# Opening the z1 stage before the last row's norm is finished

## The chip, the cores and the metric

The kernel runs on one core of one Trainium2 chip. The metric is the time of one execution on the device in microseconds (us); lower is better. The engines are named as in the profile: PE (TensorE, matmuls), PEld (its weight loads), DVE (VectorE), ACT (ScalarE), POOL (GpSimd) and SP (SyncE, which here only issues DMAs). Each engine has its own list of instructions and works through it in order; an instruction waits until the semaphores it names say that its operands are there and its buffer is free.

## The reference, cut to what matters

One block of an FNet mixer followed by a gated MLP, for x of 2048 rows by 512 columns, in float32:

```python
mod = (silu(c) @ w_mod).reshape(c.shape[0], 6, 1, -1)          # sa, ca, ga, sb, cb, gb
h = layernorm(x) * (1 + ca) + sa
x = x + ga * Real(DFT_seq(DFT_hidden(h)))                      # Cr @ a - Ci @ b
h = layernorm(x) * (1 + cb) + sb
z = gelu(h @ w_in)                                             # 2048 x 1792
z1, z2 = z[..., :896], layernorm(z[..., 896:])
g = w_sp @ z2 + b_sp                                           # w_sp is 2048 x 2048
x = x + gb * ((z1 * g) @ w_out)
```

## The kernel before, in words

Every float32 matmul is made of three matmuls on rounded parts: high by high, low by high, high by low (`matmul3`, lines 95 to 97). A high part is an ACT copy (`ah`, line 249), a low part is a DVE subtraction (`al`, line 265), each of 128 by 512 elements.

The work is a row of numbered chunks. Chunks 0 to 127 (`N2` is 128) are the DFT along the sequence: four quarters `t` of 512 output rows, in PSUM tiles `gp`. As a quarter ends, `mm_y` makes the DFT along the hidden dimension, four row tiles `yp` of 128 rows. Each row tile goes through five steps: `post_y` (DVE scales and adds x, then takes mean and variance; POOL stores x and finishes the statistics), `norm_y` (ACT applies them), `post_h` (DVE multiplies by `mod4` and adds `mod3`), `turn_h` (DVE turns the tile into `hturn`, POOL stores it to `ht_d` in DRAM with four DMAs). Chunks 128 to 155 (from `N2` to `N3`) make z1 from `ht_d` and the left half of w_in: 7 products of the Strassen-Winograd kind with 4 chunks each, tiles `z1p`, and a leftover column block `f7p` of 128 columns. Chunks 156 to 183 (`N3` to `N4`) make z2 the same way (`z2p`). Chunks 184 to 295 (from `N4`) make w_sp times z2 (`gw`), and the output product `op` follows.

The order on every engine is written by hand. In each chunk `prep(n)` emits the high part of chunk n+3 and the low part of chunk n+2, then the matmuls are emitted, then `run(n)` emits whatever `at(n, ...)` has put on that chunk's list. `prep_hi` and `prep_lo` for chunks 128 to 131 read `xb0`, the turned rows of quarters 0 and 1 that already lie in SBUF; chunks 132 to 135 read `xb1`; quarters 2 and 3 come back from `ht_d` through `load_t` into the tiles `tt2` and `tt3` of the pool `slots`, which `change_s` opens where the DFT's pools have been closed.

The place the change is about is the passage from chunk 127 to 128. There, the lists at `N2 - 0.25` hold the five steps of the last quarter's four rows, one row after the other. The first z1 chunks follow at once: `mm_z1(128)` (product 1, left pair), `mm_z1(130)` (right pair), `mm_z1(132)` (product 2, which begins with two `f7p` groups on chunks 132 and 133), and then `mm_x(0)`, the `f7p2` matmuls on `xh` and `xl`, parts of `tt2`. `empty_z1` copies a finished `z1p` tile to SBUF with ACT. `mm_x(0)` writes the PSUM bank that `f7p0` filled, so it waits for the gelu that empties it (line 670), the first gelu of the program, ahead of which ACT loads its table.

Tiles that share a tag share a ring of buffers: `row` has 6 in the pool `rows` (x rows, h rows, and in the last quarter the odd turned rows), `hturn` has one.

## Time and profile before

| | |
|---|---|
| runs shown (3) | median 950.87 us, 949.32 to 951.08 |
| the profiled execution | 949.74 us |
| its span in the trace | 948.0 us |
| PE busy | 934.8 us (99% of the span) |
| DVE busy | 737.5 us (78%) |
| ACT busy | 413.5 us (44%) |
| POOL busy | 196.2 us (21%) |
| mean granted PE clock | 0.997 |

The 1.7 us between the profiled time and the span lie outside the program's instructions. In a timeline row the columns are: start in us from the start of the span, duration in us, engine, line, operation, written tile <- read tiles, shape, count, and in brackets how long the engine was idle before it and what ended that. Matmuls overlap: one of 512 columns is listed with 0.39 us, but in an unbroken row the next starts 0.227 us later (0.203 us for 448 columns). What a wait costs is therefore read from start to start, less that step. In a waits row stand who waited, for whom, the total in us, how often, and the longest.

### The profile page before, as it was taken

The page shows a single profiled execution, that of the slowest core. Times are in us where ns is not written, and L with a number is a line of the kernel's source. Part 1 is how long each engine was busy: PE and PEld are TensorE (multiplying, and loading weights), DVE is VectorE, ACT ScalarE, POOL GpSimd, SP SyncE. Part 2 cuts the span into 40 slices and gives each one's busy share as a digit, 9 for nine tenths or more (in the row PEclk, how much of TensorE's full clock was granted, in tenths as well). Part 3 has the DMA queues.
Part 4 walks back from the last instruction along what each step waited for, and adds up shares of the span by engine and source line. Part 5 has one row for each costly group of instructions (what it writes and reads, how often), then busy time and mean ns, then how long its engine had stood idle before and what let it go on. Part 6 is the DMA issues. An engine that isn't in the chain of part 4 may idle for free.

```text
span 948.0 us, 12382 instructions
## 1 busy us (share of the span) xinstructions
PE 934.8 (99%) x4114; PEld 773.2 (82%) x4114; DVE 737.5 (78%) x1201; ACT 413.5 (44%) x725; POOL 196.2 (21%) x372
## 2 busy tenths in 40 slices
PE   8999999999999999999899999999999999999998
PEld 5888888888887888888688898888888888888886
DVE  7799957777667677866787868999799889886662
ACT  4694424232132222322577778765545444331221
POOL 2330000114544165323414211332000000000000
PEclk9999999999999999999999999999999999999999
DMA  9995752657448977994767322544555465744441
GB/s 209 221 224 122 137 145 67 167 140 195 121 120 235 325 224 213 278 336 158 230 246 271 140 82 57 149 92 102 135 131 122 101 156 126 185 101 156 180 175 56
DMA packets 236592, 157.07 MB, mean 166 GB/s; under 512 B 131472, under 2 KB 203408, under 8 KB 236400
## 3 DMA queue, kind: packets, MB, share of 16 engines
q1 hardware_dynamic: 223008, 118.65, 50.0%
q0 software_dynamic: 12128, 37.11, 10.9%
q8 instruction: 32, 0.52, 0.2%
q10 hardware_dynamic: 1392, 0.52, 0.2%
q14 instruction: 32, 0.26, 0.1%
HBM read 119.54 MB, written 36.70 MB: 165 GB/s over the span
## 4 chain that ended last, share of the span: by engine, by line
PE 86%; issue 6%; POOL 3%; DVE 3%; ACT 1%; DMA 1%; SPq 0%; POOLq 0%; DVEq 0%
PE gp L96 12%; PE gp L95 12%; PE gp L97 12%; PE gw L97 10%; PE gw L96 10%; PE gw L95 10%; PE op L97 3%; PE op L96 3%; PE op L95 3%; PE yp L97 2%; PE yp L96 2%; PE yp L95 2%; PE z2p L97 2%; PE z2p L96 2%; PE z2p L95 2%
## 5 line engine op out<-in xcount | busy, mean ns | idle before, releaser
L249 ACT ACTIVATE ah<-t 128x512 fp32r<-128x512 f32 x248 | 156.4, 631 | 373.1 <-DVE t L186 267.5
L265 DVE TENSOR_TENSOR al<-t,ah 128x512 fp32r<-128x512 f32 x248 | 166.7, 673 | 59.2 <-PE gp L96 32.8
L96 PE MATMUL gp<-al,hh 128*128 128x512 f32 x496 | 193.1, 389 | 0.9 <-DVE al L265 0.9
L95 PE MATMUL gp<-ah,hh 128*128 128x512 f32 x496 | 193.0, 389 | 0.0
L97 PE MATMUL gp<-ah,hl 128*128 128x512 f32 x496 | 193.0, 389 | 0.0
L186 DVE STREAM_TRANSPOSE t<-stage 128x512 f32<-128x512 f32 x240 | 168.6, 702 | 7.4 <-DMA stage<-in_A_dft_seq_re_dram 3.3
L97 PE MATMUL gw<-ah,bl 128*128 128x512 f32 x400 | 155.9, 390 | 0.3 <-DVE bl L806 0.3
L95 PE MATMUL gw<-ah,bh 128*128 128x512 f32 x400 | 155.7, 389 | 0.0
L96 PE MATMUL gw<-al,bh 128*128 128x512 f32 x400 | 155.6, 389 | 0.0
L96 PEld LDWEIGHTS gp<-al,hh 128*128 128x128 f32 x496 | 93.1, 188 | 20.5 <-DVE al L265 1.3
L95 PEld LDWEIGHTS gp<-ah,hh 128*128 128x128 f32 x496 | 93.1, 188 | 19.5
L97 PEld LDWEIGHTS gp<-ah,hl 128*128 128x128 f32 x496 | 93.1, 188 | 19.3
L97 PEld LDWEIGHTS gw<-ah,bl 128*128 128x128 f32 x400 | 75.1, 188 | 16.6 <-DVE bl L806 1.0
L95 PEld LDWEIGHTS gw<-ah,bh 128*128 128x128 f32 x400 | 75.1, 188 | 15.6
L96 PEld LDWEIGHTS gw<-al,bh 128*128 128x128 f32 x400 | 75.1, 188 | 15.6
L778 POOL DMA_DIRECT2D s_d<-sj x64 | 35.1, 548 | 97.0 <-DVE sj L770 81.2
L95 PE MATMUL yp<-hth,gh 128*128 128x512 f32 x128 | 49.8, 389 | 0.0
L96 PE MATMUL yp<-htl,gh 128*128 128x512 f32 x128 | 49.8, 389 | 0.0
L97 PE MATMUL yp<-hth,gl 128*128 128x512 f32 x128 | 49.8, 389 | 0.0
L569 POOL DMA_DIRECT2D ht_d<-hturn x62 | 40.9, 665 | 30.4 <-DVE hturn L565 26.2
L95 PE MATMUL op<-woh,uh 128*128 128x512 f32 x112 | 43.6, 389 | 0.0
L96 PE MATMUL op<-wol,uh 128*128 128x512 f32 x112 | 43.6, 389 | 0.0
(200 smaller groups left out, 1445.4 us busy)
## 6 DMA issues: line engine op xcount, KB each, us to landing
stage<-in_A_dft_seq_im_dram SPq DMA_DIRECT2D x64, 256.0 KB, 5.3
sj<-in_B_w_sp_dram SPq DMA_DIRECT2D x32, 512.0 KB, 7.4
s_d<-sj POOLq DMA_DIRECT2D x64, 256.0 KB, 3.7
stage<-s_d SPq DMA_DIRECT2D x128, 128.0 KB, 2.8
stage<-in_A_dft_seq_re_dram SPq DMA_DIRECT2D x60, 256.0 KB, 5.4
stage<-in_B_w_sp_dram SPq DMA_DIRECT2D x96, 128.0 KB, 3.0
wm<-in_w_mod_dram SPq DMA_DIRECT2D x16, 256.0 KB, 5.8
xr<-in_A_x_dram POOLq DMA_DIRECT2D x16, 256.0 KB, 4.6
```

Source lines behind the costliest of these rows:

```text
L95: nc.tensor.matmul(acc, ah, bh, start=first, stop=False, skip_group_check=go_on)
L96: nc.tensor.matmul(acc, ah, bl, start=False, stop=False, skip_group_check=go_on)
L97: nc.tensor.matmul(acc, al, bh, start=False, stop=last, skip_group_check=go_on)
L186: nc.vector.transpose(dst.rearrange("p (b i) -> p b i", i=32), block[:, :, 32 * k:32 * k + 32])
L249: nc.scalar.activation(AH[n], T[n], AF.Copy)
L265: nc.vector.tensor_tensor(AL[n], t, AH[n].bitcast(F32), op=ALU.subtract)
L569: eng.dma_start(v[a, i], ht[32 * a:32 * a + 32].rearrange("c (b r) -> c b r", r=32))
L778: nc.gpsimd.dma_start(s_d[m, r, g][b * P:(b + 1) * P, :], a)
```

## The change

Five things are changed.

1. `turn_h` puts the turned tile of every odd row of quarters 1 to 3 into the `row` ring. Before, only the last quarter did so, and all rows of quarters 0 to 2 shared the one `hturn` buffer.
2. In `mm_z1` the copies of the three `z1p` tiles are emitted ahead of the leftover matmuls of product 1, not behind them.
3. In the passage, the low part of chunk 131 is emitted ahead of `post_y` of the last row; `norm_y`, `post_h` and `turn_h` of the last row move behind `mm_z1(128)`, with the high parts of chunks 132 and 133 and the low part of 132 emitted between them. `change_s`, and with it the pool for `tt2`, moves behind them, and `load_t(2)` from the list of chunk 128 to that of 129.
4. The sums on w_in's right half: `form_w(6)` moves from chunk `N3` to `N2 + 26`, which is `N3 - 2`; `form_w(5)` and `form_w(4)` one chunk earlier.
5. The first eight z norms (`norm_z` on DVE and POOL, `scale_z` on ACT) move two chunks later, and `hi_b` of the first w_sp product one chunk later.

```diff
     def prep_hi(n):
-        if n >= NE:
+        if n >= NE or n in highs:
             return
+        highs.add(n)
...
-        pl, tag, n = (rows, "row", 6) if t == NQ - 1 and i % 2 else (GP_[0], "hturn", 1)
+        pl, tag, n = (rows, "row", 6) if t and i % 2 else (GP_[0], "hturn", 1)
...
+        for f in range(3):
+            empty_z1(p, gg, f)
         if p == 1:
             for kk, t in enumerate(a):
                 mm_f7(gg, kk, *t)
-        for f in range(3):
-            empty_z1(p, gg, f)
...
-                at(N2 - 0.25, post_y, t, i)
                 if i == 3:
                     at(N2 - 0.25, prep_lo, N2 + 3)
-                at(N2 - 0.25, norm_y, t, i)
+                at(N2 - 0.25, post_y, t, i)
                 if i:
                     at(N2 - 0.25, turn_h, t, i - 1)
-                at(N2 - 0.25, post_h, t, i)
+                if i < 3:
+                    at(N2 - 0.25, norm_y, t, i)
+                    at(N2 - 0.25, post_h, t, i)
...
-    change_s()
-    zout.append(w0.enter_context(pool("zout")))
-    at(N2, load_t, 2)
+    at(N2 + 1, load_t, 2)
...
+    at(N2 + 26, form_w, 6)
...
             mm_z1(n)
+            if n == N2:
+                prep_hi(N2 + 4)
+                norm_y(NQ - 1, 3)
+                prep_hi(N2 + 5)
+                prep_lo(N2 + 4)
+                post_h(NQ - 1, 3)
+                turn_h(NQ - 1, 3)
+                change_s()
+                zout.append(w0.enter_context(pool("zout")))
...
-        if p == 6:
-            at(N3, form_w, 6)
...
-    at(N3 + 6, form_w, 5)
-    at(N3 + 7, form_w, 4)
+    at(N3 + 5, form_w, 5)
+    at(N3 + 6, form_w, 4)
...
-            at(n - 4, hi_b, p, k)
+            at(n - (3 if p == 1 else 4), hi_b, p, k)
...
-                at(n - 7, norm_z, k)
-                at(n - 6, scale_z, k)
+                at(n - 5, norm_z, k)
+                at(n - 4, scale_z, k)
```

Neither PE's nor POOL's nor SP's list of instructions changes its order; on DVE and ACT the same instructions stand in another order at a few places. Three of them are shown.

ACT in the passage, before: `h2_3_3` is the last row's norm, the DMA two of its four stores, `z1_1_0x` and `z1_1_1x` the copies of product 1's left and right tiles, `ah132` to `ah134` the high parts of those chunks.

```order
L119 ACTIVATE h2_3_3_4235<-xr3_3_4183,nmry_4231,rsy_4228 128x512
L569 DMA ht_d3_83<-hturn3_3_4245 32x16x32 x2
L708 ACTIVATE z1_1_00_4302<-z1p1_00_4274 128x4x4x32
L708 ACTIVATE z1_1_01_4304<-z1p1_01_4281 128x4x4x32
L708 ACTIVATE z1_1_02_4306<-z1p1_02_4288 128x4x4x32
L249 ACTIVATE ah132_4308<-xb1_3935 128x512
L249 ACTIVATE ah133_4313<-xb1_3935 128x512
L708 ACTIVATE z1_1_10_4350<-z1p1_10_4322 128x4x4x32
L708 ACTIVATE z1_1_11_4352<-z1p1_11_4329 128x4x4x32
L708 ACTIVATE z1_1_12_4354<-z1p1_12_4336 128x4x4x32
L249 ACTIVATE ah134_4356<-xb1_3935 128x512
```

The same stretch of ACT's list in the changed kernel:

```order
L710 ACTIVATE z1_1_00_4262<-z1p1_00_4241 128x4x4x32
L710 ACTIVATE z1_1_01_4264<-z1p1_01_4248 128x4x4x32
L710 ACTIVATE z1_1_02_4266<-z1p1_02_4255 128x4x4x32
L252 ACTIVATE ah132_4275<-xb1_3935 128x512
L119 ACTIVATE h2_3_3_4277<-xr3_3_4183,nmry_4233,rsy_4230 128x512
L252 ACTIVATE ah133_4279<-xb1_3935 128x512
L571 DMA ht_d3_83<-hturn3_3_4285 32x16x32 x2
L710 ACTIVATE z1_1_10_4343<-z1p1_10_4322 128x4x4x32
L710 ACTIVATE z1_1_11_4345<-z1p1_11_4329 128x4x4x32
L710 ACTIVATE z1_1_12_4347<-z1p1_12_4336 128x4x4x32
L252 ACTIVATE ah134_4356<-xb1_3935 128x512
```

The left tiles' copies and `ah132` now stand ahead of the last row's norm, and `ah133` ahead of the two stores; the right tiles' copies and `ah134` still stand behind the stores.

DVE in the passage, before: `y3_3`, `xr3_3`, `bsty` and `mvy` are `post_y` of the last row, `hturn3_2` and `hturn3_3` the turned third and fourth row.

```order
L546 TENSOR_TENSOR y3_3_4220<-yp3_3_0_4099,mod2_1784 128x512
L547 TENSOR_TENSOR xr3_3_4183<-y3_3_4220,xr3_3_4183 128x512
L103 BN_STATS bsty_4224<-xr3_3_4183 128x6
L105 BN_AGGR mvy_4226<-bsty_4224 128x2
L265 TENSOR_TENSOR al131_4233<-xb0_3845,ah131_4188 128x512
L565 STREAM_TRANSPOSE hturn3_2_4237<-h2_3_2_4205 128x512
L557 TENSOR_TENSOR h2_3_3_4235<-h2_3_3_4235,mod4_2060 128x512
L558 TENSOR_TENSOR h2_3_3_4235<-h2_3_3_4235,mod3_2222 128x512
L565 STREAM_TRANSPOSE hturn3_3_4245<-h2_3_3_4235 128x512
L265 TENSOR_TENSOR al132_4315<-xb1_3935,ah132_4308 128x512
L265 TENSOR_TENSOR al133_4317<-xb1_3935,ah133_4313 128x512
```

And in the changed kernel:

```order
L267 TENSOR_TENSOR al131_4220<-xb0_3845,ah131_4188 128x512
L548 TENSOR_TENSOR y3_3_4222<-yp3_3_0_4099,mod2_1784 128x512
L549 TENSOR_TENSOR xr3_3_4183<-y3_3_4222,xr3_3_4183 128x512
L103 BN_STATS bsty_4226<-xr3_3_4183 128x6
L105 BN_AGGR mvy_4228<-bsty_4226 128x2
L567 STREAM_TRANSPOSE hturn3_2_4235<-h2_3_2_4211 128x512
L267 TENSOR_TENSOR al132_4281<-xb1_3935,ah132_4275 128x512
L559 TENSOR_TENSOR h2_3_3_4277<-h2_3_3_4277,mod4_2060 128x512
L560 TENSOR_TENSOR h2_3_3_4277<-h2_3_3_4277,mod3_2222 128x512
L567 STREAM_TRANSPOSE hturn3_3_4285<-h2_3_3_4277 128x512
L267 TENSOR_TENSOR al133_4317<-xb1_3935,ah133_4279 128x512
```

`al131` moved ahead of the last row's four statistics instructions, `al132` ahead of its last three; `al133` kept its place behind the last turn.

DVE in the last z2 product, four chunks ahead of `N4`, before: `t180` and `t181` are sums for chunks 180 and 181, `bstz` and `mvz` the statistics of the first z norm (`norm_z`), `z2_12` the first of four sums of a finished PSUM tile.

```order
L232 TENSOR_TENSOR t180_5436<-xb1_3935,s2_00_4430 128x512
L644 TENSOR_TENSOR wj2_5398<-w2_4310,wj2_5398 128x2x448
L103 BN_STATS bstz_5441<-z2_0_5158 128x6 x2
L105 BN_AGGR mvz_5444<-bstz_5441 128x2
L232 TENSOR_TENSOR t181_5451<-xb1_3935,s2_01_4435 128x512
L265 TENSOR_TENSOR al180_5455<-t180_5436,ah180_5438 128x512
L265 TENSOR_TENSOR al181_5457<-t181_5451,ah181_5453 128x512
L746 TENSOR_TENSOR z2_12_5028<-z2p5_4_5354,z2_12_5028 128x448
```

And in the changed kernel:

```order
L232 TENSOR_TENSOR t180_5436<-xb1_3935,s2_00_4430 128x512
L646 TENSOR_TENSOR wj2_5398<-w2_4314,wj2_5398 128x2x448
L232 TENSOR_TENSOR t181_5441<-xb1_3935,s2_01_4435 128x512
L267 TENSOR_TENSOR al180_5445<-t180_5436,ah180_5438 128x512
L267 TENSOR_TENSOR al181_5447<-t181_5441,ah181_5443 128x512
L748 TENSOR_TENSOR z2_12_5028<-z2p5_4_5354,z2_12_5028 128x448
```

The first norm's statistics left this place; they stand one list further on, behind `t182`, and ACT's `scale_z(0)` moved with them, from behind `ah181` to behind `ah183`.

More of the change, by code (lines that the diff above doesn't have):

```diff
@@ L234, in form_t @@
         return {7: c, 4: d, 5: a, 3: b}[p]
+    highs, lows = set(), set()
     def prep_hi(n):
-        if n >= NE:
+        if n >= NE or n in highs:
             return
+        highs.add(n)
         if N2 <= n < N4:
@@ L252, in prep_hi @@
             load(b + 2)
-    lows = set()
     def prep_lo(n):
@@ L1041, in fnet_gmlp_kernel @@
                     at(N2 - 0.25, prep, N2)
-                at(N2 - 0.25, post_y, t, i)
                 if i == 3:
                     at(N2 - 0.25, prep_lo, N2 + 3)
-                at(N2 - 0.25, norm_y, t, i)
+                at(N2 - 0.25, post_y, t, i)
                 if i:
                     at(N2 - 0.25, turn_h, t, i - 1)
-                at(N2 - 0.25, post_h, t, i)
+                if i < 3:
+                    at(N2 - 0.25, norm_y, t, i)
+                    at(N2 - 0.25, post_h, t, i)
                 if i < 2:
                     at(N2 - 0.25, load_xr, t, i + 2)
-                for f, *a in (((hi_v, 1), (lo_v, 1)), ((make_w7, 0),), ((hi_v, 2), (lo_v, 2), (make_w7, 1)), ((turn_h, t, 3),))[i]:
+                for f, *a in (((hi_v, 1), (lo_v, 1)), ((make_w7, 0),), ((hi_v, 2), (lo_v, 2), (make_w7, 1)), ())[i]:
                     at(N2 - 0.25, f, *a)
```

## The prediction

> **What bounds the kernel now.** I read the page's busy times first, then the waits of PE, then PE's timeline around each wait, then the engines that end them.

> ```profile
> PE 934.8 (99%) x4114; PEld 773.2 (82%) x4114; DVE 737.5 (78%) x1201; ACT 413.5 (44%) x725; POOL 196.2 (21%) x372
> ```

> PE is busy for 99% of the span and the change leaves its instructions and their order alone. So time can only be won or lost where PE waits. Its waits are few; the largest behind the start (who, for whom, total us, times, longest):

> ```profile
> PE f7p L95 <- ACT ah L249: 2.3, 1, 2.3
> PE z2p L95 <- ACT ah L249: 1.7, 2, 1.4
> ...
> PE z1p L96 <- DVE al L265: 1.0, 1, 1.0
> ```

> These, and two smaller ones shown below, lie at places that the change touches: `gp` in quarter 2, `z1p` and `f7p` in the passage, `z2p` at both ends of that stage, `gw` at its start. I cost them in order of time. Times below are those of the trace before; what earlier terms move is added at the end only.

> **Turned rows in the ring.** PE and DVE in quarter 2:

> ```profile
> 293.45 0.39 PE L95 MATMUL gp<-ah,hh 128*128 128x512 f32 x1
> 294.75 0.50 PE L96 MATMUL gp<-al,hh 128*128 128x512 f32 x1 [0.91 <-DVE al L265]
> ```

> ```profile
> 292.82 0.71 DVE L565 STREAM_TRANSPOSE hturn<-h 128x512 f32<-128x512 f32 x1 [3.92 <-DMA ht_d<-hturn]
> ```

> DVE stands for 3.92 us until the one buffer's stores have landed, and behind it stands the low part that PE lacks. PE loses 294.75 - 293.45 - 0.23 = 1.07 us. With odd rows in the ring the fourth turn needs no landing of the third, and 3.92 us of wait ahead of a loss of 1.07 leave a wide margin. The ring's other users, x rows loaded through POOL, have had this pattern in the last quarter already. Term: -1.07.

> **The passage.** PE there:

> ```profile
> 455.86 0.39 PE L95 MATMUL z1p<-ah,vj 128*128 128x512 f32 x1
> 457.21 0.50 PE L96 MATMUL z1p<-al,vj 128*128 128x512 f32 x1 [0.96 <-DVE al L265]
> 457.55 0.40 PE L97 MATMUL z1p<-ah,vj 128*128 128x512 f32 x1
> ...
> 461.69 0.39 PE L97 MATMUL f7p<-ah,w 128*128 128x512 f32 x1
> 464.39 0.49 PE L95 MATMUL f7p<-ah,w 128*128 128x512 f32 x1 [2.31 <-ACT ah L249]
> ...
> 468.58 0.40 PE L95 MATMUL z1p<-ah,vj 128*128 128x512 f32 x1
> ...
> 472.02 0.39 PE L95 MATMUL f7p<-xh,w 128*128 128x512 f32 x1
> ```

> From 455.86 to 457.55 two steps take 1.69, a loss of 1.24. From 461.69 to 468.58 ten steps of 0.227 take 6.89, a loss of 4.62. Together 5.86. The second loss is not the wait alone: the granted clock fell.

> ```profile
> 461.59:465.00 3.41, 0.98 (x4) 0.25 (x2) 0.63 (x2) 2.75 (x6) 1.29 (x2) 1.00 0.51 96
> 465.00:468.41 3.41, 3.30 (x8) 2.62 (x9) 3.38 (x6) 3.41 (x8) 0.00 (x0) 0.50 0.39 132
> 587.88:591.29 3.41, 1.92 (x9) 1.32 (x9) 2.41 (x5) 3.41 (x7) 1.33 (x3) 1.00 0.49 110
> ```

> (Columns: stretch, length, busy us and count of PE, PEld, DVE, ACT, POOL, granted clock, DMA share, GB/s.) Half clock ran from 465.00 to 468.41, after a stretch of 3.41 us in which PE was busy for 0.98 (29%). A stretch of the same length with 1.92 (56%) was not followed by it. Half clock cost 3.41 / 2 = 1.7 of the 5.86.

> What ends the two waits is ACT and DVE working for the last row first:

> ```profile
> 458.25 0.81 ACT L119 ACTIVATE h<-xr,nmry,rsy 128x512 f32<-128x512 f32 x1 [5.56 <-POOL nmry L115]
> 461.30 0.91 ACTq L569 DMA_DIRECT2D ht_d<-hturn  x2
> 462.25 1.57 ACT L708 ACTIVATE z<-z1p 128x512 f32<-128x512 f32 x3 [3.18 <-PE f7p L97]
> 464.73 1.58 ACT L708 ACTIVATE z<-z1p 128x512 f32<-128x512 f32 x3
> 470.43 0.60 ACT L670 ACTIVATE z1o<-f7p 128x512 f32<-128x512 f32 x1
> ```

> ```profile
> 446.56 0.69 DVE L265 TENSOR_TENSOR al<-xb,ah 128x512 fp32r<-128x512 f32 x1
> ...
> 459.10 0.69 DVE L557 TENSOR_TENSOR h<-h,mod 128x512 f32<-128x512 f32 x1 [1.32 <-ACT h L119]
> ...
> 460.55 0.71 DVE L565 STREAM_TRANSPOSE hturn<-h 128x512 f32<-128x512 f32 x1
> ```

> `al131` now stands four DVE instructions earlier and is done some 2 us before PE asks: the 1.24 go. `ah132` runs in the 5.56 us for which ACT waits at 458.25, and `al132` fills DVE's 1.32 at 459.10, since one low part is 0.69 long and lets the next start after 0.60 (two in a row take 1.29, below). Both cost nothing there. But `al131` pushes the last row's chain back by 0.60: turn at 461.15, stores at 461.90.

> What is late next, then. First `al133`, behind that turn: it starts some 0.6 later, at 461.8, and is done at 462.5. PE, without the 1.24, asks for it at 461.69 - 1.24 + 5 x 0.227 = 461.59: a new wait of 0.90. Then the `f7p2` matmuls, which stood at 472.02 and need the bank that the first gelu frees. From the second trio of copies (464.73) to that gelu's end (471.03) ACT works without a hole, 6.30 us: copies, two high parts, two `xh`, weights, table load, gelu. In the new order the right tiles' copies follow the stores directly, at 461.90 + 0.95 = 462.85, so the bank is free at 469.15 and PE goes on at 469.20. PE itself is there at 472.02 - 5.86 + 0.90 = 467.06, and waits about 2.1. So the passage is 472.02 - 469.20 = 2.8 shorter, less 0.1 for the slower first matmul behind a wait (457.21 to 457.55 is 0.34, not 0.23): -2.7. Two waits become two others, and the copies' place ahead of the leftover matmuls buys nothing, because the right ones wait for the stores. A sum that took the removed waits alone would give 5.9.

> That holds at full clock. The new wait leaves PE idle for about 2.0 us, so the fullest stretch of 3.41 around it has PE busy for 41%, between the 29% and the 56% above, and it lies wholly in one stretch in (3.41 - 2.0) / 3.41 = 41% of phases. I give half clock about 2 in 10, at a price of 1.7. [...]

> **w_in's sums.** At the start of z2:

> ```profile
> 530.57 0.95 ACT L640 ACTIVATE wj<-w 128x896 fp32r<-128x896 f32 x1 [3.09 <-DVE w L629]
> ```

> ```profile
> 533.23 0.36 PE L97 MATMUL z2p<-wj,al 128*128 128x448 f32 x1
> ...
> 534.86 0.36 PE L95 MATMUL z2p<-wj,ah 128*128 128x448 f32 x1
> ```

> ```profile
> 526.91 1.29 DVE L265 TENSOR_TENSOR al<-t,ah 128x512 fp32r<-128x512 f32 x2 [0.18 <-ACT ah L249]
> ...
> 529.45 1.08 DVE L629 TENSOR_TENSOR w<-w 128x896 f32<-128x896 f32 x1
> ```

> PE loses 534.86 - 533.23 - 4 x 0.203 = 0.82 behind ACT's 3.09 us wait for `form_w(6)`. Two chunks earlier the sum is ready and that wait is gone. On DVE its 1.08 now stand ahead of the low parts of chunks 158 and 159. Those ended at 527.6 and 528.2; PE began on that half 24 matmuls of 0.203 before 533.43, at 528.6, and read them from 529.0 and 529.6: 1.4 to spare, 0.3 left. Term: -0.8; if the cover were gone, up to 0.8 of it would come back.

> **z's norms.** The end of z2:

> ```profile
> 587.59 0.36 PE L97 MATMUL z2p<-wj,al 128*128 128x448 f32 x1
> ...
> 590.62 0.37 PE L96 MATMUL z2p<-wj,ah 128*128 128x448 f32 x1
> ...
> 595.64 0.50 PE L97 MATMUL gw<-ah,bl 128*128 128x512 f32 x1 [0.33 <-DVE bl L806]
> ```

> ```profile
> 583.95 1.14 ACT L119 ACTIVATE z<-z,nmrz,rsz 128x896 f32<-128x896 f32 x1 [0.89 <-POOL nmrz L115]
> ...
> 588.73 1.14 ACT L249 ACTIVATE ah<-t 128x512 fp32r<-128x512 f32 x2
> ...
> 590.29 1.12 ACT L119 ACTIVATE z<-z,nmrz,rsz 128x896 f32<-128x896 f32 x1
> ```

> ```profile
> 580.37 1.15 DVE L103 BATCH_NORM_STATS2 bstz<-z 128x6 f32<-128x448 f32 x2
> ```

> Loss: 590.62 - 587.59 - 5 x 0.203 = 2.0, and at 595.64 the 0.33 shown and 0.16 of overlap, 0.5, with 0.1 behind it: 2.6. Ahead of `ah182`, at 588.73, the change takes away a wait of 0.89 and a scale of 1.14 on ACT, and 1.15 of statistics on DVE ahead of that; `ah182` comes 1.2 to 1.9 earlier, at 586.8 to 587.5, done half of 1.14 later, by 588.1 at the latest, against PE's 587.79. The 2.0 shrink to 0.3. But the norm now stands between `ah183` and the first `bh`: its scale, then the copies and high parts that were there before, and `bl` comes behind them. Before, the scale began 583.95 - 580.37 = 3.6 behind the start of its statistics. Now these stand behind four sums of 0.55 and `t182` (0.6). The sums move with the pairs, and start at 582.5 to 583.1; so the scale starts at 588.9 to 589.5, where the second norm's stood at 590.29, with the same copies and high parts behind it and one `bh` of 0.5 more ahead of the last `al`. `bl` comes 0.3 to 0.9 earlier, up to 1.5 if POOL's part of the 3.6 is shorter here. PE asks 1.7 earlier, so its wait grows from 0.5 to between 0.7 and 1.9, and `bl` sets the term: between -0.3 and -1.5; I take -0.7, inside the nearer span. The other seven norms are still scaled four chunks ahead of their use, 48 matmuls of 0.227 or 10.9 us.

> **The sum.** -1.07 - 2.7 - 0.8 - 0.7 = -5.3. The profiled execution took 949.74 (span 948.0 and 1.7 around it), 1.1 under the median shown: 944.4 for it, 945.6 against the median of 950.87. POOL and SP keep their order, so no transfer is issued behind another that it stood ahead of.

> **Rivals.**
> - The new wait cools the clock: +1.7, 947.3. For it the 29% stretch, against it the 56% one. Still faster.
> - The passage is not shortened, because `tt2` comes late. SP's loads wait for buffers:

> ```profile
> SPq L205 <- PE yp L97: 17.4, 1, 17.4
> SPq L205 <- DMA ht_d<-hturn: 16.3, 1, 16.3
> ```

> The first is `load_t(2)`, which waits for `yp` matmuls, the second `load_t(3)`, issued at 465.9 when the last turned row has landed. The pool for both is now opened behind that row's turn. If the first load must wait like the second, `tt2` lands some 3.5 us later, at 469.4; 3.8 of ACT's 6.30 follow, and PE goes on at 473.3, 1.3 later than before instead of 2.8 earlier. Sum: 1.07 + 0.8 + 0.7 - 1.3 = 1.3 gained, 949.6: within 0.2%, which is 1.9 us and about what a measurement of this kernel can tell from no change. Against it: what it waited for in the end was PE, which the matmuls' operands under those buffers explain, and these stay where they were.
> - Slower, by DVE in the first w_sp product, where the norms now fall two chunks later and run into the second eight:

> ```profile
> 597.00:610.78 13.78, 13.78 (x63) 11.38 (x62) 13.18 (x25) 9.38 (x14) 4.75 (x9) 1.00 0.48 109
> ```

> DVE is busy for 13.18 of 13.78. That leaves 0.24 in each pair of chunks (24 matmuls of 0.227, 5.4 us). One more norm's statistics in each of the 8 pairs, 1.15, would put 0.9 a pair on PE, 7.3 in all: 945.6 + 7.3 = 952.9. It decides once more than 5.3 of it reach PE. Against it: of the first eight norms three instead of four now stand ahead of that product, so one is added, not eight, and PE waits nowhere in that stretch.

> **How the numbers follow.** Forecast 0.65; clock 0.19; late `tt2` 0.09; DVE 0.07. Faster by over 0.2%: 0.84; within: 0.09; slower: 0.07. The forecast's own bounds are the norm term (0.4 up, 0.8 down) and the runs' spread (949.32 to 951.08). The range takes the clock rival in with the norm term at its worst end, 945.6 + 1.7 + 0.4 and 0.9 of spread, 948.6; below, the norm term at its best and the profiled execution for the base, 943.6, with 0.4 for new waits taken too long: 943.2.

> **What would show it.** Right: no PE wait in quarter 2; PE's first z1 wait on `al133`, about 0.9; a wait of about 2 on the gelu ahead of `f7p2`, with full clock behind it; none at `form_w(6)`; a wait on `bl` of about 1.3 at the first `gw`. Wrong: half clock after the passage, SP's first `L205` waiting on `hturn`, or PE waiting for `al` in the first w_sp product.

## The result and the profile after

The changed kernel takes 945.69 us (median of 4 runs, 944.42 to 946.25), the kernel before, in the same comparison, 950.8 (4 runs, 949.32 to 951.08): a ratio of 0.9948, 95% interval 0.993 to 0.9965. The forecast was 945.6.

The profiled execution took 945.85, with a span of 944.1. Its busy times are those of before within 2 us:

```profile
PE 932.9 (99%) x4114; PEld 773.4 (82%) x4114; DVE 739.0 (78%) x1201; ACT 414.5 (44%) x725; POOL 196.2 (21%) x372
```

So the waits tell the story. PE's list of waits (who, for whom, total us, times, longest):

```profile
PE f7p L95 <- ACT z1o L672: 1.8, 1, 1.8
PE gp L449 <- ACT ah L252: 1.6, 1, 1.6
PE busyp L354 <- DVE busy L293: 1.5, 1, 1.5
PE gw L97 <- DVE bl L808: 1.1, 1, 1.1
PE f7p L96 <- DVE al L267: 0.6, 1, 0.6
```

The second and third are at the start of the program, where the first loads land. The waits of before for `gp` in quarter 2 (0.9), `f7p` for `ah` (2.3), `z1p` (1.0) and `z2p` (1.7) are gone. Three stand in their place: `f7p` for the first gelu, 1.8; `f7p` for `al133`, 0.6; `gw` for `bl`, 1.1. PE's timeline at the first two:

```profile
459.51 0.39 PE L95 MATMUL f7p<-ah,w 128*128 128x512 f32 x1
460.50 0.50 PE L96 MATMUL f7p<-al,w 128*128 128x512 f32 x1 [0.61 <-DVE al L267]
...
467.18 0.50 PE L95 MATMUL f7p<-xh,w 128*128 128x512 f32 x1 [1.84 <-ACT z1o L672]
```

From start to start the first costs 460.50 - 459.51 - 0.23 = 0.76. What holds the second is ACT's list:

```profile
459.90 0.89 ACTq L571 DMA_DIRECT2D ht_d<-hturn  x2
460.84 1.58 ACT L710 ACTIVATE z<-z1p 128x512 f32<-128x512 f32 x3 [2.64 <-DVE al L267]
462.28 1.16 ACT L252 ACTIVATE ah<-xb 128x512 fp32r<-128x512 f32 x2
463.33 1.16 ACT L211 ACTIVATE xh<-tt 128x512 fp32r<-128x512 f32 x2
464.37 0.85 ACT L606 ACTIVATE vj<-w1e 128x768 fp32r<-128x768 f32 x1
465.24 1.28 ACT L672 ACT_TABLE_LOAD   x1
466.53 0.60 ACT L672 ACTIVATE z1o<-f7p 128x512 f32<-128x512 f32 x1
```

The 2.64 us are ACT waiting, until 459.90, for the last turned row, and issuing its two stores. Only then it works without a hole from 460.84 to 467.13, 6.29 us, to the end of the gelu that PE needs. And here the clock did fall, which the prediction had named as a sign of being wrong (stretch, length, busy us and count of PE, PEld, DVE, ACT, POOL, granted clock, DMA share, GB/s):

```profile
465.29:468.70 3.41, 1.57 (x8) 1.26 (x8) 3.38 (x6) 3.40 (x6) 1.28 (x3) 1.00 0.87 264
468.70:472.11 3.41, 3.41 (x10) 2.65 (x9) 1.71 (x4) 3.41 (x8) 0.91 (x2) 0.50 0.82 238
```

SP's two loads of turned rows waited as before, the first for PE and not for the rows' landing:

```profile
SPq L205 <- PE yp L97: 17.4, 1, 17.4
SPq L205 <- DMA ht_d<-hturn: 16.9, 1, 16.9
```

To see where the time went I cut each span at PE marks and took the times between them. In us, worked out from the starts of PE's matmuls in each trace (from PE's first matmul on; "passage" is from the first `z1p` matmul of chunk 128 to the first of `mm_x(0)`, "its end" the 30 matmuls behind that, "end of z2" the last 28 `z2p`):

| stretch | before | after | difference |
|---|---|---|---|
| up to PE's 25th `gp` | 14.32 | 13.74 | -0.58 |
| DFT | 433.89 | 432.68 | -1.21 |
| passage | 22.28 | 19.23 | -3.05 |
| its end | 6.80 | 8.59 | +1.79 |
| rest of z1 | 44.88 | 44.88 | 0 |
| first 56 `z2p` | 12.17 | 11.38 | -0.79 |
| middle of z2 | 51.12 | 52.08 | +0.96 |
| end of z2 | 7.71 | 5.85 | -1.86 |
| first 12 `gw` | 3.36 | 4.23 | +0.87 |
| from there to PE's last matmul | 345.48 | 345.44 | -0.04 |

That adds up to the 3.9 by which the two spans differ. The first row is no term of the change: that stretch took between 13.7 and 15.8 in the profiles of this document, with no order to it. The medians differ by 5.1; the experiments say why one pair of profiles shows less.

### The profile page after: what moved, and what is told of

Read it like the earlier page. It is cut to its first block, busy times and chain, and to the rows that moved or that the text cites. A ratio compares the mean times of both kernels' runs of the same rounds, so it can differ in the third digit from the quotient of the medians.

```text
span 944.1 us, 12382 instructions
## 1 busy us (share of the span) xinstructions
PE 932.9 (99%) x4114; PEld 773.4 (82%) x4114; DVE 739.0 (78%) x1201; ACT 414.5 (44%) x725; POOL 196.2 (21%) x372
## 4 chain that ended last, share of the span: by engine, by line
PE 94%; DVE 2%; ACT 1%; DMA 1%; POOL 1%; issue 1%; SPq 0%; ACTq 0%; DVEq 0%; POOLq 0%
PE gp L97 12%; PE gp L95 12%; PE gp L96 12%; PE gw L97 10%; PE gw L96 10%; PE gw L95 10%; PE op L97 3%; PE op L96 3%; PE op L95 3%; PE yp L96 2%; PE yp L95 2%; PE yp L97 2%; PE z2p L97 2%; PE z2p L95 2%; PE z2p L96 2%; PE z1p L96 2%
## 5 line engine op out<-in xcount | busy, mean ns | idle before, releaser
L95 PE MATMUL gp<-ah,hh 128*128 128x512 f32 x496 | 193.0, 389 | 0.0
L97 PE MATMUL gp<-ah,hl 128*128 128x512 f32 x496 | 193.0, 389 | 0.0
L96 PE MATMUL gp<-al,hh 128*128 128x512 f32 x496 | 193.0, 389 | 0.0
L97 PE MATMUL gw<-ah,bl 128*128 128x512 f32 x400 | 155.9, 390 | 1.1 <-DVE bl L808 1.1
L95 PE MATMUL gw<-ah,bh 128*128 128x512 f32 x400 | 155.7, 389 | 0.0
L96 PE MATMUL gw<-al,bh 128*128 128x512 f32 x400 | 155.7, 389 | 0.0
L95 PEld LDWEIGHTS gp<-ah,hh 128*128 128x128 f32 x496 | 93.1, 188 | 19.3
L97 PEld LDWEIGHTS gp<-ah,hl 128*128 128x128 f32 x496 | 93.1, 188 | 19.3
L96 PEld LDWEIGHTS gp<-al,hh 128*128 128x128 f32 x496 | 93.1, 188 | 19.3
L97 PEld LDWEIGHTS gw<-ah,bl 128*128 128x128 f32 x400 | 75.1, 188 | 17.3 <-DVE bl L808 1.7
L95 PEld LDWEIGHTS gw<-ah,bh 128*128 128x128 f32 x400 | 75.1, 188 | 15.7 <-ACT bh L803 0.2
L96 PEld LDWEIGHTS gw<-al,bh 128*128 128x128 f32 x400 | 75.1, 188 | 15.5
L97 PE MATMUL yp<-hth,gl 128*128 128x512 f32 x128 | 49.8, 389 | 0.0
L95 PE MATMUL yp<-hth,gh 128*128 128x512 f32 x128 | 49.8, 389 | 0.0
L96 PE MATMUL yp<-htl,gh 128*128 128x512 f32 x128 | 49.8, 389 | 0.0
L97 PE MATMUL op<-woh,ul 128*128 128x512 f32 x112 | 43.6, 389 | 0.0
L95 PE MATMUL op<-woh,uh 128*128 128x512 f32 x112 | 43.6, 389 | 0.0
```

Of the source, the lines that this page charges most:

```text
L95: nc.tensor.matmul(acc, ah, bh, start=first, stop=False, skip_group_check=go_on)
L96: nc.tensor.matmul(acc, ah, bl, start=False, stop=False, skip_group_check=go_on)
L97: nc.tensor.matmul(acc, al, bh, start=False, stop=last, skip_group_check=go_on)
```

## The experiments

**The ring alone, the passage alone, the sums alone, the norms alone.** Each is the kernel before with one part of the change; together they are the whole of it.

```diff
# e1: the ring
-        pl, tag, n = (rows, "row", 6) if t == NQ - 1 and i % 2 else (GP_[0], "hturn", 1)
+        pl, tag, n = (rows, "row", 6) if t and i % 2 else (GP_[0], "hturn", 1)
# e2: the passage (parts 2 and 3 of the change)
+            if n == N2:
+                prep_hi(N2 + 4)
+                norm_y(NQ - 1, 3)
...
# e3: w_in's sums (part 4)
+    at(N2 + 26, form_w, 6)
...
# e4: z's norms (part 5)
-            at(n - 4, hi_b, p, k)
+            at(n - (3 if p == 1 else 4), hi_b, p, k)
-                at(n - 7, norm_z, k)
-                at(n - 6, scale_z, k)
+                at(n - 5, norm_z, k)
+                at(n - 4, scale_z, k)
```

> The kernel before with the odd turned rows of quarters 1 to 3 in the ring, and nothing else. If the one buffer held up the low part in quarter 2: 1.1 us faster, no wait of PE in quarter 2, and in the passage the same waits as before (2.3 and 1.0 us, and half clock behind them). Rival, that the low part was late for another reason, or that the ring's x loads now hold up POOL: under 0.3 us either way, or a new wait of PE in quarters 2 or 3.

> The kernel before with the new order of the passage alone (low part of 131 and high parts of 132 and 133 earlier, copies ahead of the leftover matmuls, the last row's norm behind the first z1 matmuls). By the sum of the prediction: 2.7 us faster in executions whose clock stays, about 1.0 in those in which the wait for the first gelu halves it; PE waits about 0.6 to 0.9 for the low part of 133 and about 1.8 for the gelu, and quarter 2 still loses 1.07. Rival, that the waits only changed their place: within 0.5 us of the kernel before whatever the clock does.

> The kernel before with the sums of w_in's right half earlier, alone. If ACT's wait for that sum was the whole loss at the start of z2: 0.8 us faster, no wait of PE there. Rival, from the trace of the changed kernel, in which the 448-column matmuls behind that place start every 206.7 ns and not every 202.7: if it is the missing wait that sets the slower pace, some 270 matmuls by 4 ns give 1.1 us back, and this kernel is 0.3 us slower, not faster.

> The kernel before with the later norms of z alone. By the prediction 0.7 us faster (0.3 to 1.5): no wait of 1.4 us at the second half of the last z2 product, a wait for the first low part of the w_sp product that grows from 0.3 to over 1 us. Rival, that the one takes all of the other: within 0.2 us. The pace of the 448-column matmuls should stay at 202.7 ns if the sums set it.

Measured, against the kernel before at 951.88 us (26 runs, 949.43 to 955.18):

| | median, range | ratio, 95% | what its own stretches became |
|---|---|---|---|
| ring | 949.29, 948.05 to 949.62 | 0.9968, 0.9956 to 0.998 | DFT 432.66 |
| passage | 950.63, 948.13 to 954.53 | 0.999, 0.9976 to 1.0004 | passage 19.26, its end 8.54 |
| sums | 949.82, 948.95 to 953.11 | 0.9979, 0.9969 to 0.9989 | first 56 `z2p` 11.34 |
| norms | 949.76, 949.29 to 954.7 | 0.9984, 0.9972 to 0.9996 | end of z2 6.12, first `gw` 4.19 |

The last three runs keep the one turned-row buffer, and their PE rows in quarter 2 were a surprise. The passage alone, then the sums alone, then the norms alone:

```profile
295.12 0.50 PE L96 MATMUL gp<-al,hh 128*128 128x512 f32 x1 [1.48 <-DVE al L267]
```

```profile
296.22 0.60 PE L96 MATMUL gp<-al,hh 128*128 128x512 f32 x1 [2.14 <-DVE al L265]
```

```profile
296.41 0.50 PE L96 MATMUL gp<-al,hh 128*128 128x512 f32 x1 [2.49 <-DVE al L265]
```

On the same instructions PE waited 0.91 in the profile that I costed, and 1.48, 2.14 and 2.49 here; in the run with the sums half clock followed as well. DVE's rows show why: how long it stands depends on when the stores land. The last of the four stores ahead of the fourth turn took 3.3 us from its issue to its landing in the profile that I costed (289.42 to 292.69) and 4.6 in the norms alone (289.79 to 294.35). DVE in the norms alone:

```profile
286.06 0.71 DVE L565 STREAM_TRANSPOSE hturn<-h 128x512 f32<-128x512 f32 x1 [5.13 <-DMA ht_d<-hturn]
...
294.47 0.71 DVE L565 STREAM_TRANSPOSE hturn<-h 128x512 f32<-128x512 f32 x1 [5.21 <-DMA ht_d<-hturn]
```

The second wait was 3.92 in the profile that I costed. With the ring alone no turn of that quarter waits (its passage had the waits of before, 2.3 and 1.0, but against the expectation no half clock):

```profile
280.25 0.70 DVE L565 STREAM_TRANSPOSE hturn<-h 128x512 f32<-128x512 f32 x1
...
285.40 0.70 DVE L565 STREAM_TRANSPOSE hturn<-h 128x512 f32<-128x512 f32 x1
```

The DFT then takes 432.66, and 432.68 in the changed kernel, where without the ring it takes 433.89, 434.67, 435.50 and 436.72 (the last with half clock). So the ring is worth 1.2 to 4.1, not 1.07. The 5 runs with it scatter over 1.6 us and the 26 before over 5.8, which fits, though 5 runs show less of a scatter than 26. The sums gave 0.8, the norms 1.6 less 0.8, both within 0.3 of the ledger of the whole change. By their ratios the four would gain 3.0, 1.0, 2.0 and 1.5, together 7.5, where the whole change gained 5.1: parts of about a microsecond are not to be read from runs that scatter by five, and I use the stretches.

**Does the copies' place in `mm_z1` matter?** The changed kernel with the copies behind the leftover matmuls again, as before:

```diff
-        for f in range(3):
-            empty_z1(p, gg, f)
         if p == 1:
             for kk, t in enumerate(a):
                 mm_f7(gg, kk, *t)
+        for f in range(3):
+            empty_z1(p, gg, f)
```

> The changed kernel with the copies of the z1 tiles behind the leftover matmuls again. The prediction says that their place buys nothing, because the right tiles' copies stand behind the last row's stores: the same waits in the passage within 0.1 us, and the time of the changed kernel. Rival, that the copies gain the six leftover matmuls they no longer wait for: the wait for the first gelu is 1.4 us longer.

Measured: 944.7 (943.78 to 945.31), ratio 0.9916 (0.9896 to 0.9936). Passage 19.27 against 19.23, the same three waits (1.9, 0.6 and 1.1), no half clock behind the gelu wait in this profile: its end is 6.94. Part 2 of the change moves no wait.

**What holds the gelu: its table, or the stores ahead of it?** Three runs. In one an early gelu, on a small tile of its own, loads the table at chunk 60. In one POOL issues all four stores of the last row. One has both, and `bh` of the first block another chunk later.

```diff
# e6: the table early
+    first_gelu = cpool.tile([P, ND], F32, name="first_gelu")
+    at(60, nc.scalar.activation, first_gelu, ones[:, :ND], AF.Gelu_apprx_tanh)
# e7: the stores on POOL
-            eng = nc.scalar if (t, i) == (NQ - 1, 3) and a > 1 else nc.gpsimd
-            eng.dma_start(v[a, i], ...)
+            nc.gpsimd.dma_start(v[a, i], ...)
# e8: both, and
-            at(n - (3 if p == 1 else 4), hi_b, p, k)
+            at(n - ((2 if k == 0 else 3) if p == 1 else 4), hi_b, p, k)
```

> The changed kernel with one small gelu in the DFT, so that ACT's table for gelu is loaded long before the first real one. If ACT's row of work between the last stores and that gelu sets the wait: the 1.8 us shrink by the load's 1.3 to about 0.6, and no half clock follows; 1.3 us faster than executions of the changed kernel at full clock, 3.0 than those with half clock. Rival, that the low parts of xh on DVE are as late: under 0.5 us.

> The changed kernel with all four stores of the last turned row on POOL, none on ACT. If the right tiles' copies are late because ACT stands at these stores until the last turn is done: the copies start when their matmuls end, some 2 us earlier, and the wait of 1.8 for the first gelu shrinks to under 0.3, with no half clock behind it. POOL's stores end 1.3 us later and with them the loads of quarter 3, which cost nothing unless a wait at the second xh appears (rival: the 1.8 return there).

> The changed kernel with the early table, all stores of the last row on POOL, and the first high part of z2 one chunk later, behind the two high parts of the w_sp product. No wait for the first gelu, the one of 0.6 for the low part of 133 stays; at the first w_sp matmuls the wait of 1.1 for the low part splits into about 0.6 for the high part and 0.3 for the low one, 0.4 less in all: 2.3 us faster than the changed kernel at full clock, 4 than with half clock. Rival, that the slower pace of the 448-column matmuls comes with the ring: then all four kernels of this set show 206.7 ns, as the changed kernel and the ring alone did.

Measured: the early table 958.1 (956.45 to 959.94), ratio 1.006 (1.0044 to 1.0076); the stores on POOL 941.67 (941.08 to 942.35), ratio 0.9889 (0.9874 to 0.9904); both 956.85 (955.5 to 957.01), ratio 1.0043 (1.0029 to 1.0058).

Either is enough to take most of the wait away, the stores all of it. With them on POOL, ACT goes on without waiting for the turned row:

```profile
458.16 0.62 ACT L252 ACTIVATE ah<-xb 128x512 fp32r<-128x512 f32 x1
458.68 1.55 ACT L709 ACTIVATE z<-z1p 128x512 f32<-128x512 f32 x3
...
465.08 0.60 ACT L671 ACTIVATE z1o<-f7p 128x512 f32<-128x512 f32 x1
```

and PE's waits lose the one for the gelu:

```profile
PE gw L97 <- DVE bl L807: 1.1, 1, 1.1
PE f7p L96 <- DVE al L267: 0.6, 1, 0.6
```

The passage falls from 19.23 to 17.25 and no half clock follows. With the early table the gelu wait fell to 0.4 and the passage to 17.83. But the stretch behind the first 12 `gw` took 353.6 instead of 345.44 in both kernels with that table, and the DFT 438.23 and 438.54 instead of 432.68. The later `bh` of the third kernel split the wait of 1.1 at the first `gw` into 0.3 and 0.2, where 0.6 and 0.3 were expected. Either the early gelu does this, or its tile of 16 bytes a partition, which I take to move the buffers behind it. That, and whether the remaining waits can go, was left for the last four runs.

**The table without a tile, the tile without the table, a larger tile, and the best order.** The first three change the changed kernel, the last the one with the stores on POOL.

```diff
# e11: the table, result into columns of a tile that is there and does not use them
+    at(60, nc.scalar.activation, cols_[:, 36:40], ones[:, :ND], AF.Gelu_apprx_tanh)
# e10: 16 bytes a partition more, no gelu (e12: 256 bytes, F32 x 64)
+    pad = cpool.tile([P, ND], F32, name="pad")
+    nc.gpsimd.memset(pad, 0.0)
# e9: on top of the stores on POOL
                 prep_lo(N2 + 4)
+                prep_lo(N2 + 5)
...
-            at(n - (3 if p == 1 else 4), hi_b, p, k)
+            at(n - ((2 if k == 0 else 3) if p == 1 else 4), hi_b, p, k)
```

> The changed kernel with the early gelu of chunk 60, its result written into unused columns of a tile that is there already, so that no buffer moves. Theory placement: gw rest stays at 345.4; the wait of f7p for gelu falls from 1.84 to about 0.4 as in the first early-gelu run, z1 to mm_x from 19.2 to 17.8, no half clock: 944.0 us (943 to 945) against 945.7. Rival, the table: gw rest 353.6 again, 957 us.

> The changed kernel with the 16-byte tile of the early-gelu run, filled once by POOL, and no early gelu. Theory placement: the tile moves every buffer allocated above it by 16 or 32 bytes, and transfers and matmuls run at another pace from the start: the transfers between 100 and 150 us at a DMA share of about 0.8 (0.52 in the changed kernel), gw rest 353.6 against 345.4, time 957 to 959 us. Rival, the early table load: without the gelu nothing is slow, 945.7 us and gw rest 345.4.

> The changed kernel with a tile of 256 bytes instead of 16, no early gelu. If any move of the buffers is slow: 957 us, gw rest 353.6. If only a move that is no multiple of 64 bytes is: 945.7, gw rest 345.4. Something between, if transfers and matmuls want different multiples: the DMA share between 100 and 150 us (0.52 or 0.81) and gw rest then differ in which of the two they resemble.

> The kernel with the last row's four stores on POOL, and two more moves: bh of the first w_sp block one chunk later, and the low part of block 133 ahead of the last row's norm as well. Against that kernel (941.67 us): the first gw waits no longer for bl (stages z2 308-gw and gw +12 together 9.68 against 10.34 in the run that had the later bh, so -0.66), and if the order alone made the wait of f7p for al 133 (0.61 idle, 0.77 from start to start), z1 to mm_x falls from 17.25 to 16.5. Sum -1.4: 940.2 us, range 939.4 to 941.0. Rival: the early low part delays h and with it z1o, and the time comes back as a wait of f7p for gelu: z1 to mm_x stays at 17.2 or above, 941.0 us.

Measured: the table alone 942.89 (942.78 to 943.5), ratio 0.9909 (0.9892 to 0.9925); the small tile alone 961.19 (960.14 to 962.85), ratio 1.0103 (1.0087 to 1.0118); the 256 bytes 944.47 (943.47 to 944.91), ratio 0.9924 (0.9909 to 0.9939). So the tile's 16 bytes cost the 12 us and more, and the table nothing: with it in old columns PE waits for the gelu 0.4,

```profile
PE gw L97 <- DVE bl L808: 1.1, 1, 1.1
PE f7p L96 <- DVE al L267: 0.6, 1, 0.6
PE f7p L95 <- ACT z1o L672: 0.4, 1, 0.4
```

the passage is 17.81, and no half clock follows. 942.89 is 1.1 below the 944.0 I expected. The 256 bytes cost nothing, so not every added tile is slow; sizes between the two were not tried, so no run shows whether the 64 bytes of the expectation are the line. The same 50 us on the clock, in the DFT, in the changed kernel, with 16 bytes, and with 256 (columns as above):

```profile
100.00:150.00 50.00, 50.00 (x222) 41.44 (x221) 32.70 (x53) 17.22 (x30) 2.15 (x4) 1.00 0.52 121
```

```profile
100.00:150.00 50.00, 50.00 (x221) 41.18 (x220) 36.73 (x59) 18.56 (x32) 2.12 (x4) 1.00 0.77 142
```

```profile
100.00:150.00 50.00, 50.00 (x223) 41.40 (x222) 32.94 (x53) 17.11 (x29) 2.15 (x4) 1.00 0.53 121
```

With 16 bytes the DMA engines are busy for 0.77 of the time to move 142 GB/s, without them for 0.52 to move 121: a byte takes 26% longer. The two stretches do not hold the same transfers. Over the whole program the largest queue does (queue, kind, packets, MB, share of 16 engines), in the changed kernel and with 16 bytes:

```profile
q1 hardware_dynamic: 223008, 118.65, 49.9%
```

```profile
q1 hardware_dynamic: 223008, 118.65, 60.1%
```

By the spans, 944.1 and 961.1, its packets took 23% longer. At which bytes the transfers start, no view shows, and so why 16 bytes cost this and 256 do not stays open. PE is slower too, in two ways. In the DFT its matmuls keep their step of 227 ns and most of what is lost are waits ahead of 60 us, the longest 1.8 for a low part, with half clock behind it in this profile. In the w_sp product the step itself grows. The `gw` group by line, in the changed kernel and with 16 bytes (count, busy us, mean ns of one):

```profile
L97 PE MATMUL gw<-ah,bl 128*128 128x512 f32 x400 | 155.9, 390 | 1.1 <-DVE bl L808 1.1
```

```profile
L97 PE MATMUL gw<-ah,bl 128*128 128x512 f32 x400 | 158.2, 396 | 1.1 <-DVE bl L808 1.1
```

From start to start the median step of the 1200 `gw` matmuls is 227 ns in the first and 234 in the second. That 7 ns, 8 us in all, comes with the tile; through which operand was not tried, and so why PE slows stays open.

The best order came to 941.91 (941.2 to 942.67), ratio 0.9899 (0.9884 to 0.9914), where the stores on POOL alone had 941.67. The early low part took `al133`'s wait away, and the gelu wait came back in its place; `bh` a chunk later changed one wait into two smaller ones:

```profile
PE f7p L95 <- ACT z1o L671: 1.2, 1, 1.2
...
PE gw L95 <- ACT bh L802: 0.3, 1, 0.3
PE gw L97 <- DVE bl L807: 0.2, 1, 0.2
```

DVE now waits for `ah133` with the last row behind it, and w1e's sum, which ACT needs ahead of the gelu, comes later:

```profile
458.34 0.69 DVE L267 TENSOR_TENSOR al<-xb,ah 128x512 fp32r<-128x512 f32 x1 [1.54 <-ACT ah L252]
...
461.98 0.96 DVE L594 TENSOR_TENSOR w1e<-w 128x768 f32<-128x768 f32 x1
```

The passage is 17.71 against 17.25 (+0.46), the end of z2 with the first `gw` 9.90 against 10.34 (-0.44): a draw, and the first part went as the rival in the expectation had it. The kernel with the stores on POOL, 941.67, is the best found: about 10 under the kernel before in its comparison (951.8), and 4.0 under the changed one by their medians.

## Why the prediction was right, and where its sizes were off

**The waits.** All five steps came as described: no PE wait in quarter 2; `al133` late; the gelu's bank as the next thing late; none at `form_w(6)`; `bl` late at the first `gw`. The "copies' place buys nothing" held as well. Half clock behind the gelu wait, where the prediction had said full clock, came as well (below). Sizes: `al133` 0.76 for 0.90; gelu wait 1.84 idle, for "about 2.0"; ACT's unbroken run 6.29 for 6.30, begun at 460.84 behind the stores.

**The ring term, -1.07, was too small.** Its step "PE loses 1.07" took one execution for all. Four executions without the ring lose 1.2, 2.0, 2.8 and 4.1 in the DFT against the 432.67 with it (the last with half clock). The margin I gave ("a wide margin") was right for what the ring removes; that the landing of stores varies by over a microsecond was in no row I looked at, and only the 1.8 us by which the runs shown differed could have hinted at it.

**The passage term, -2.7, was too large.** I subtracted an after at full clock from a before that carried half clock. Without half clock on either side the passage and its end are 28.3 before (21.40 + 6.95 with the ring alone, 21.36 + 6.93 with the norms alone) and 26.2 after (19.23 + 6.95 with the 256 bytes): -2.1. The step that failed is "the passage is 472.02 - 469.20 shorter": 472.02 was itself 0.9 late by half clock (22.28 against 21.38). Of the 1.7 before paid 0.8 with its end counted in, since PE then waited less for the bank (not at all, against 0.4 with the ring or the norms alone); the sums alone, where half clock lasted two stretches, paid 1.9. Against the one profile that I costed, 29.1, the term was sound: -2.9 at full clock.

**The clock rival was underrated.** It had "half clock about 2 in 10" at 1.7. With this gelu wait half clock came in three profiles of five (after, passage alone, 16 bytes; not with the late copies nor with 256 bytes), at 1.6 to 1.7 (its end 8.54 to 8.61 against 6.94). The price was right. What told the three from the two is where the wait fell. In each trace the recorded changes of the clock lie whole stretches of 3.413 us apart (full clock ahead of the half clock lasts 457.39 in the trace of before and 464.21 in that of after, 134 and 136 of them), so all stretches can be counted off from them. Where one stretch held the whole wait, PE was busy in it for 1.56 or 1.57 (46%), and half clock followed, three times of three. Where a boundary cut the wait, PE was busy for 1.80 (53%, late copies) and 1.87 (55%, 256 bytes), and full clock stayed, twice of two. The prediction's share of phases, 41%, was about right; what it had too low was the chance that such a stretch is enough, about one half. A sharp line in PE's listed busy time does not come out, though. The first of these stretches (the norms alone) was not followed by half clock, the second (16 bytes, early in the DFT) was, the third (early table and stores on POOL) was not:

```profile
462.21:465.62 3.41, 1.52 (x7) 0.94 (x5) 0.70 (x1) 1.72 (x4) 1.73 (x3) 1.00 0.43 79
```

```profile
53.16:56.58 3.42, 1.63 (x7) 1.05 (x7) 1.64 (x3) 0.83 (x2) 0.00 (x0) 1.00 1.07 213
```

```profile
54.30:57.71 3.41, 1.63 (x7) 1.36 (x8) 2.97 (x5) 2.17 (x4) 0.00 (x0) 1.00 1.07 205
```

So in these profiles the change from one to the other lies at 45% to 48%, and the prediction's 56% was a loose upper bound. A wait of 1.84 was enough for half clock, as the one of 2.31 was in the profile that I costed. With the passage of before it came in two profiles of four (before and the sums alone), so the medians contain it on both sides, which is why this rival was not a case apart from the forecast.

**Sums and norms.** -0.8 forecast, -0.79 measured; the cover behind it (the low parts of chunks 158 and 159) held. Norms -0.7 forecast, -0.76 alone and -0.99 in the whole change.

**The other rivals.** `tt2` was not late: SP's first load ended its wait with PE. DVE in the first w_sp product: no PE wait there, and the stretch from the 12th `gw` on stayed at 345.44.

**The sum.** On the medians -5.1 for -5.3. That the medians meet the forecast of 945.6 within 0.1 is luck, two errors that cancel: some 1 to 2 more from the ring, and less from the passage, 0.6 by its size and more where half clock follows. The profiled pair shows 3.9 because before had its shortest ring wait, after had half clock at the full price, and after's z2 ran slower by 0.96, for a reason that stays open (below).

## What to carry to other kernels

A wait for stores to land is priced from several executions: here PE's loss behind it went from 0.9 to 2.5, where the waits in the passage repeated to 0.1 us. Runs that scatter are a reason to look for such a wait. Two stores issued by ACT held the copies behind them for 2.64 us, until the turned row was there and the stores were issued: moving them from ACT to POOL took 2.0 us off a passage that the whole reordering around them had shortened by 2.1. And a small tile is not free: one of 16 bytes a partition cost 15.5 us, so a scratch result belongs in columns that are already there, or in a tile padded to 256 bytes, the one size tried here that cost nothing.

## What the runs showed of the hardware that was not expected

```profile
535.00:575.00 40.00, 40.00 (x195) 1.00 0.25 80
```

```profile
535.00:575.00 40.00, 40.00 (x199) 1.00 0.25 79
```

The slower pace came in the profiles of the changed kernel, the ring alone, the table in old columns, the 256 bytes and, at 206.1, the three with the 16-byte tile; the faster in those of before, the passage, sums and norms alone, the late copies, the stores on POOL and the best order. DMA share and rate are alike, so they do not tell the two apart. It is worth 0.9 us. The ring does not set it, since three kernels with the ring had the faster pace; no run separates its cause, and it may differ between executions of one kernel.
